# Two attention units scored singly instead of as a pair, and one value tile issued ahead of the mask build

## The chip, the cores and the metric

One core of one Trainium2 chip. Names in the profiles: PE is the matrix engine (PEld its weight loads), ACT the scalar engine, DVE the vector engine, POOL the general engine, which also issues most of the loads here; PSUM is the memory that PE writes to. The metric is the device time of one execution in microseconds (us), lower is better. The time of an execution is some 1.7 us longer than the profile's span.

## The reference, cut to what matters

```python
# q, k, v: (8 batches, 8 heads, 576 positions, 64), float32
scores = q @ k.T / 8
scores = where(abs(i - j) <= 32, scores, -1e9)      # sliding window
attn = softmax(scores) @ v
x = attn, heads side by side: (4608, 512)
h = x @ w_in                                        # w_in (512, 2048)
out = (h / (1 + exp(-1.702 * h))) @ w_out           # w_out (2048, 512)
```

## The kernel before

The 4608 rows are cut into 36 units of 128 rows, each of two blocks of 64 queries. A block needs 128 keys: the first block of a unit finds their values in the unit's own value tile (`ve`), the second in a shifted copy (`vo`) that takes 64 rows from each of two neighbouring tiles. From unit 10 on two units are scored together ("pair"), because their middle keys are shared. The order of instructions on each engine is the order of the program.

```python
def scores(self, u, ...):                 # single form; 32 products for 4 head pairs
    sc[u] = two PSUM banks (eo = even / odd heads), p[u] = [128, 2, 8, 64]
    ...
                        nc.tensor.matmul(sc[eo][lo:lo + 64, n, :], self.kT[r, hp, at:at + 64],
                                         self.qT[r, ..., q0:q0 + 16], ...)      # 64 x 64 x 64
    for eo in range(2):
        nc.scalar.activation(p[:, eo, cols], sc[eo][:, cols], AF.Exp, scale=self.scale)

def band(self, u, ...):                   # 2 mask products of 128 x 512, one for each eo
    ...

def scores_pair(self, a, kinds):          # 40 products, most of them 64 x 64 x 128
    sc = four PSUM banks (g = half of the head pairs, eo), each for BOTH units
    ...
    for (g, eo), src in sc.items():       # order (0,0) (0,1) (1,0) (1,1)
        nc.scalar.activation(p[:, eo, 2 * g:2 * g + 2], src, AF.Exp, scale=self.scale)

def band_pair(self, a):                   # 2 mask products of 128 x 1024: all heads of one eo, both units
    ...

def values_pair(self, us, kinds):         # 16 products for the first unit, then 16 for the second
    ...

def head(self):                           # the opening
    ... keys and queries of the first 512 rows are loaded
    for m in range(2):
        self.load_v(m)
    self.setup_mask()                     # POOL: one memset, four affine selects
    self.load_v(2, 0, 64)                 # the half tile
    for c in "kq":
        self.load_edge(c)
    self.load_w_in(0)
    self.load_v(2, 64); self.load_v(3); self.load_v(4, 0, 64)
    for c in range(1, 4):
        self.load_w_in(c)                 # second, third, fourth quarter of w_in
    ...
        self.layer1(0, 2)                 # needs the second quarter
        self.x_T(2, "t")
        self.layer1(0, 3)
        self.x_T(3, "o")
        self.layer1(0, 4)                 # the first step that needs the third quarter
        for d in range(4):
            self.layer1(1, d)             # need the first and second quarter

def window_4(self):
    ...
    run(l1)                               # last step of layer 1
    self.scores_pair(10, "aaaa")
    self.band_pair(10)                    # then window 5: layer 2 of unit 6, values_pair((10, 11)), scores_pair(12)
```

The softmax here doesn't subtract the row's maximum and nothing guards it: scores larger than these inputs give would overflow.

Of the kernel before, what the change touches and what calls it, by code (L numbers as in the profile page):

```python
# [23 lines left out]
RING = 1536  # L24
# [3 lines left out]
class _Kernel:  # L28
# [206 lines left out]
    def scores(self, u, hps=range(4), kinds="aa"):  # L235

        nc = self.nc
        if u not in self.p:
            self.sc[u] = [self.bank(kinds[eo], [128, 8, SQ], F32, f"sc{eo}") for eo in range(2)]
            self.p[u] = self.work.tile([128, 2, 8, SQ], BF16, name="p", tag="p", bufs=4)  # L240
        sc, p = self.sc[u], self.p[u]
        for hp in hps:
            for blk in range(2):
                n = 2 * hp + blk
                k0 = (128 * u + 64 * blk) % RING
                q0 = (128 * u + 64 * blk + 32) % RING // JT
                for half in range(2):
                    lo, at = 64 * half, k0 + 64 * (half ^ blk)
                    for eo in range(2):
                        r = slice(eo * 64, eo * 64 + 64)  # L250
                        nc.tensor.matmul(sc[eo][lo:lo + 64, n, :], self.kT[r, hp, at:at + 64],  # L251
                                         self.qT[r, JT * hp:JT * hp + JT, q0:q0 + 16],
                                         start=(hp in (0, hps[0]) and blk == 0), stop=(hp == hps[-1] and blk == 1))
        cols = slice(2 * hps[0], 2 * hps[-1] + 2)
        for eo in range(2):
            nc.scalar.activation(p[:, eo, cols], sc[eo][:, cols], AF.Exp, scale=self.scale)  # L256
# [76 lines left out]
    def values_pair(self, us, kinds):  # L333

        nc, D = self.nc, self.D
        acc = [self.bank(kind, [128, (7, 7, 2)[i], D + 1], F32, f"pv{i}") for i, kind in enumerate(kinds)]
        p = self.p.pop(us[0])
        for i, u in enumerate(us):
            for h in range(self.H):
                out, n = (acc[i], h) if h < 7 else (acc[2], i)  # L340
                for blk in range(2):
                    vt = (self.ve, self.vo)[blk][u % NV]
                    nc.tensor.matmul(out[blk * 64:blk * 64 + 64, n, :], p[:, h % 2, h // 2, 2 * i + blk, :],  # L343
                                     vt[:, h, :D + 1], start=(h in (0, 7)), stop=(h in (6, 7)))
            self.acc[u] = (acc[i], acc[2], i)

# [117 lines left out]
    def head(self):  # L464

        nc, dve, act = self.nc, self.nc.vector, self.nc.scalar
# [5 lines left out]
                self.load_heads(0, c, h)  # L472
        for m in range(2):
            self.load_v(m)
        self.setup_mask()
        self.load_v(2, 0, 64)
        for c in "kq":
            self.load_edge(c)
        self.load_w_in(0)
# [149 lines left out]
    def window_4(self):  # L629

        nc, dve, act = self.nc, self.nc.vector, self.nc.scalar
        l2 = [(lambda u=u, i=i: self.layer2(u, i, "oh"[u % 2], (dve, act)[u % 2])) for u in (4, 5) for i in range(4)]
        l1 = [(lambda d=d: self.layer1(3, d)) for d in range(8)]

        def run(lst, n=1):
            for _ in range(n):
                lst.pop(0)()

        self.scores(7)
        self.scores(8)  # L640
        self.scores(9, kinds="th")
        self.keys_X(13)
        self.keys_X(14)
        run(l2, 3)
        self.band(7)
        run(l2)
        self.band(8)
        self.values(7)
        self.norm(7)
        self.gelu_table()  # L650
        self.band(9)
        run(l2, 3)
        self.values(8)
        self.values(9)
        self.x_T(7, "t", act)
        self.norm(8)
        self.x_T(8)
        self.norm(9)
        self.x_T(9)
        self.loads(4)  # L660
        run(l2)
        run(l1, 2)
        for hp in range(4):
            self.pair_heads("q", 3, hp, dve)
        run(l1, 1)
        for hp in range(4):
            self.queries_T(3, hp, "t", act)
            run(l1)
        self.queries_wrap(3)
        self.feed(4)  # L670
        run(l1)
        self.scores_pair(10, "aaaa")
        self.band_pair(10)

    def window(self, w):

# [106 lines left out]
```

## Time and profile before

| Profile of the kernel before (span 306.2 us) | us |
|---|---|
| half value tile landed | 15.21 |
| third quarter of w_in landed | 24.66 |
| PE starts the step that needs it | 24.90 |
| first score product of unit 10 | 80.67 |
| first score product of unit 12 | 86.25 |
| from there to the end | 219.95 |

Landings are from the trace's completion records: a transfer is landed when the last of its 16 transfer engines has reported. The other rows are starts of PE instructions. The table splits the run into an opening (to unit 10), the stretch that part 1 changes (unit 10 to unit 12: 5.58 us), and the rest.

### The profile page before, as it was taken

How to read it: one execution, taken by the hardware profiler on the slowest of the kernel's cores; microseconds unless marked ns; L12 is line 12 of the kernel's file. 1: busy time of each engine (PE TensorE's matmuls, PEld its weight loads, DVE VectorE, ACT ScalarE, POOL GpSimd, SP SyncE). 2: the span in 40 equal slices, each digit the busy share in tenths (PEclk: the TensorE clock that was granted, in tenths of full speed). 3: DMA queues.
4: the chain of work that ended last, by engine and by line, in shares of the span. 5: the costliest groups of instructions: out<-in, count | busy, mean ns of one | idle time of the engine just before them, and what ended most of it. 6: DMA issues, size and time to landing. Idle time of an engine off the chain costs nothing.

```text
span 306.2 us, 8062 instructions
## 1 busy us (share of the span) xinstructions
PE 295.0 (96%) x3405; PEld 204.7 (67%) x3405; DVE 132.2 (43%) x389; ACT 181.3 (59%) x310; POOL 128.5 (42%) x186
## 2 busy tenths in 40 slices
PE   8689999999999999999999999999999999999992
PEld 5469765867657676767676767676767676766852
DVE  3763178766280627072707270717070708140011
ACT  3585554795857575757575757575756567414410
POOL 8873454796325282627252625252331301130120
PEclk9979999999999999999999999999999999999997
DMA  7999999999999999999999999999999525151112
GB/s 133 162 193 205 197 186 178 174 166 154 161 167 142 106 117 146 139 141 126 153 163 126 121 147 181 108 119 154 130 66 89 57 48 72 34 65 41 37 31 72
DMA packets 130324, 38.33 MB, mean 125 GB/s; under 512 B 111280, under 2 KB 128048, under 8 KB 130288
## 3 DMA queue, kind: packets, MB, share of 16 engines
q0 software_dynamic: 90032, 27.46, 95.5%
q1 hardware_dynamic: 40112, 10.30, 36.9%
q8 instruction: 26, 0.43, 0.6%
q14 instruction: 10, 0.08, 0.1%
q10 hardware_dynamic: 144, 0.07, 0.1%
HBM read 36.96 MB, written 9.44 MB: 152 GB/s over the span
## 4 chain that ended last, share of the span: by engine, by line
PE 90%; ACT 2%; POOL 2%; DMA 2%; DVE 1%; issue 0%; POOLq 0%; ACTq 0%
PE h_ps L395 40%; PE o_ps L419 39%; PE pv L343 3%; PE sc L285 2%; DMA ve<-in_v_dram 2%; PE tp L170 1%; PE o_ps L444 1%; PE pv L329 1%; PE sc L251 1%; PE tp L380 1%; ACT g L389 1%; POOL ve L142 1%; POOL ks L136 1%; ACT pp L289 1%; POOL qs L136 0%; POOL mask L97 0%
## 5 line engine op out<-in xcount | busy, mean ns | idle before, releaser
L395 PE MATMUL h_ps<-xT,w_in_sb 128*128 128x256 bf16 (+1 forms) x1168 | 130.6, 271 | 0.0
L419 PE MATMUL o_ps<-w_out_sb,g 128*128 128x512 bf16 x560 | 127.8, 379 | 0.0
L395 PEld LDWEIGHTS <-w_in_sb 128*128 128x128 bf16 x1168 | 112.3, 98 | 16.2 <-DVE xT L108 0.3
L389 ACT ACTIVATE g<-h_ps 128x512 bf16<-128x512 f32 x142 | 84.7, 597 | 60.8 <-PE h_ps L395 60.7
L431 POOL DMA_DIRECT2D out_dram<-o_sb x70 | 44.1, 634 | 148.1 <-DVE rec L353 73.7
L419 PEld LDWEIGHTS <-g 128*128 128x128 bf16 x560 | 53.0, 98 | 57.8
L108 DVE COPY o_sb<-o_ps 128x512 f32<-128x512 f32 x34 | 23.4, 690 | 126.1 <-PE o_ps L419 126.1
L289 ACT ACTIVATE pp<-sc 128x512 bf16<-128x512 f32 x48 | 24.8, 602 | 25.3 <-PE sc L285 25.3
L142 POOL DMA_DIRECT2D ve<-in_v_dram x41 | 35.5, 869 | 9.1 <-DMA w_out_sb<-in_moe_w_out_dram 3.6
L149 POOL DMA_DIRECT2D kn<-in_k_dram x27 | 23.4, 872 | 2.8 <-DMA w_out_sb<-in_moe_w_out_dram 1.5
L108 DVE COPY vo<-ve 64x528 bf16<-64x528 bf16 x69 | 22.0, 319 | 2.2 <-DMA ve<-in_v_dram 0.3
L354 DVE TENSOR_TENSOR x<-pv,rec 128x448 bf16<-128x448 f32 (+1 forms) x52 | 22.1, 425 | 1.9
L452 ACT ACT_TABLE_LOAD x13 | 16.7, 1283 | 0.2
L108 ACT COPY qT<-tp 128x512 bf16<-128x512 bf16 (+1 forms) x16 | 9.1, 569 | 9.2 <-PE tp L170 6.3
L455 ACT ACT_TABLE_LOAD x11 | 14.1, 1283 | 0.2
L136 POOL DMA_DIRECT2D qs<-in_q_dram x17 | 12.2, 727 | 4.5 <-DMA w_out_sb<-in_moe_w_out_dram 1.6
L256 ACT ACTIVATE p<-sc 128x512 bf16<-128x512 f32 (+1 forms) x24 | 10.8, 530 | 2.7 <-PE sc L251 2.7
L343 PEld LDWEIGHTS <-pp 128*64 128x64 bf16 x416 | 7.8, 110 | 6.2 <-issue 5.1
L108 DVE COPY kT<-tp 128x512 bf16<-128x512 bf16 (+1 forms) x13 | 8.5, 659 | 6.0 <-PE tp L170 4.4
L108 DVE COPY qc<-qs 128x512 bf16<-128x512 bf16 x32 | 9.2, 331 | 2.0 <-DMA qs<-in_q_dram 2.0
L306 DVE TENSOR_TENSOR pp<-pp,mask 128x1024 bf16<-128x1024 bf16 x14 | 9.0, 684 | 2.3 <-ACT pp L289 2.3
L343 PE MATMUL pv<-ve,pp 128*64 128x65 bf16 x208 | 9.3, 196 | 0.5 <-DVE pp L306 0.4
(74 smaller groups left out, 180.3 us busy)
## 6 DMA issues: line engine op xcount, KB each, us to landing
out_dram<-o_sb POOLq DMA_DIRECT2D x70, 128.0 KB, 5.8
ve<-in_v_dram POOLq DMA_DIRECT2D x31, 128.0 KB, 8.0
kn<-in_k_dram POOLq DMA_DIRECT2D x21, 128.0 KB, 8.1
w_in_sb<-in_moe_w_in_dram POOLq DMA_DIRECT2D x4, 512.0 KB, 9.0
w_out_sb<-in_moe_w_out_dram POOLq DMA_DIRECT2D x4, 512.0 KB, 13.2
qs<-in_q_dram POOLq DMA_DIRECT2D x2, 448.0 KB, 14.7
qs<-in_q_dram POOLq DMA_DIRECT2D x3, 256.0 KB, 7.7
qs<-in_q_dram POOLq DMA_DIRECT2D x2, 384.0 KB, 11.7
```

Source lines behind the costliest of these rows:

```text
L108: (eng.copy if eng is self.nc.scalar else eng.tensor_copy)(out, in_)
L136: self.nc.gpsimd.dma_start(self.stage[key][off // JT:(off + m) // JT, lo:hi, :], src[b, lo:hi, s:s + m, :].rearrange("h (p j) d -> p h (j ...
L142: self.nc.gpsimd.dma_start(self.ve[m % NV][at:at + n, :, :self.D], self.v[b, :, s:s + n, :].rearrange("h s d -> s h d"))
L149: self.nc.gpsimd.dma_start(kn[off:off + n], self.k[b, :, s:s + n, :].rearrange("h s d -> s h d"))
L289: nc.scalar.activation(p[:, eo, 2 * g:2 * g + 2], src, AF.Exp, scale=self.scale)
L343: nc.tensor.matmul(out[blk * 64:blk * 64 + 64, n, :], p[:, h % 2, h // 2, 2 * i + blk, :], vt[:, h, :D + 1], start=(h in (0, 7)), stop=(h ...
L354: nc.vector.tensor_mul(x[:, hs, :], src[:, :, :D], rec[:, hs, :].to_broadcast([128, hs.stop - hs.start, D]))
L389: self.nc.scalar.activation(self.g[t][:, 2 * d:2 * d + 2, :], hps, AF.Gelu_apprx_sigmoid)
L395: self.nc.tensor.matmul(hps[:, i, cols], self.w_in_sb[:, kr, ff * 128:(ff + 1) * 128], self.xT[t][:, kr, cols], start=(first and i == 0 an ...
L419: nc.tensor.matmul(o_ps, self.g[t][:, ff, s * 128:(s + 1) * 128], self.w_out_sb[:, ff, :], start=(ff == 0), stop=(ff == self.NFF - 1))
L431: self.nc.gpsimd.dma_start(self.out[row + 64 * blk:row + 64 * blk + 64, :].rearrange("(s j) f -> j s f", j=JT), o_sb[64 * blk:64 * blk + 64])
L452: self.nc.scalar.activation(self.spark, self.spark, AF.Gelu_apprx_sigmoid)
```

## The change

Part 1: units 10 and 11 use the single form (needs a wrap of the key ring, and `values_pair` takes two softmax tiles). The intent is that unit 10 can be masked before unit 11 is through the exponentials. Part 2: the half value tile is issued ahead of the mask build, so that it lands earlier.

```diff
-                    lo, at = 64 * half, k0 + 64 * (half ^ blk)
+                    lo, at = 64 * half, (k0 + 64 * (half ^ blk)) % RING
... values_pair:
+        pair = us[1] not in self.p
         p = self.p.pop(us[0])
         for i, u in enumerate(us):
+            if i and not pair:
+                p = self.p.pop(u)
...
-                    nc.tensor.matmul(out[...], p[:, h % 2, h // 2, 2 * i + blk, :],
+                    pq = p[:, h % 2, h // 2, 2 * i + blk, :] if pair else p[:, h % 2, h // 2 * 2 + blk, :]
+                    nc.tensor.matmul(out[...], pq,
... head:
+        self.load_v(2, 0, 64)
         self.setup_mask()
-        self.load_v(2, 0, 64)
... window_4:
-        self.scores_pair(10, "aaaa")
-        self.band_pair(10)
+        for u in (10, 11):
+            self.scores(u)
+            self.band(u)
```

More of the change, by code (lines that the diff above doesn't have):

```diff
@@ L342, in values_pair @@
                     vt = (self.ve, self.vo)[blk][u % NV]
-                    nc.tensor.matmul(out[blk * 64:blk * 64 + 64, n, :], p[:, h % 2, h // 2, 2 * i + blk, :],
+                    pq = p[:, h % 2, h // 2, 2 * i + blk, :] if pair else p[:, h % 2, h // 2 * 2 + blk, :]
+                    nc.tensor.matmul(out[blk * 64:blk * 64 + 64, n, :], pq,
                                      vt[:, h, :D + 1], start=(h in (0, 7)), stop=(h in (6, 7)))
```

## The prediction

> **What bounds the kernel now.** I read the page first, then the chain that ended last in order of time, then the timeline of the two places that the change touches. The page, parts 1, 2 and 4:
>
> ```profile
> PE 295.0 (96%) x3405; PEld 204.7 (67%) x3405; DVE 132.2 (43%) x389; ACT 181.3 (59%) x310; POOL 128.5 (42%) x186
> ...
> PE   8689999999999999999999999999999999999992
> ...
> PE 90%; ACT 2%; POOL 2%; DMA 2%; DVE 1%; issue 0%; POOLq 0%; ACTq 0%
> ```
>
> PE is on the chain for 90% of the span. In the 40 slices (7.66 us each) it is below 9 only in the first three. So a change can shorten the run only where PE still stands idle. Busy time on the other engines is free.
>
> From about 90 us there is nothing to win: the stretch 90.10 to 105.33 (one window of two units) shows PE busy for all of its 15.23 us.
>
> ```profile
> 90.10:105.33 15.23, 15.23 (x170) 10.44 (x169) 5.86 (x16) 9.81 (x17) 6.13 (x8) 1.00 1.45 126
> ```
>
> The columns are length, then busy us (and instructions) of PE, PEld, DVE, ACT and POOL. The PE clock of 1.00 says it is not throttled. Because PE is dense from here to the end, whatever is saved before 90 us arrives whole at the end.
>
> The chain just before shows the place where units 10 and 11 are scored (columns: start us, us, what):
>
> ```profile
> 80.78 0.60 ACT g L389
> ...
> 81.39 1.28 ACT L289
> ...
> 82.69 1.58 ACT pp L289 x3
> ...
> 84.30 1.30 DVE pp L306 x2
> ...
> 85.64 0.67 PE pv L343 x30
> 86.31 0.60 PE sc L285 x30
> 86.91 3.56 PE o_ps L419 x16
> ```
>
> Here the chain leaves PE: last gelu, table load, exponentials, mask products, and only then PE's value products. Meanwhile PE runs the 16 layer-2 products of unit 6. The last of them starts at 84.52, and at 216 ns apart PE is free at 84.73. The timeline shows it waiting for the mask products:
>
> ```profile
> 84.30 1.29 DVE L306 TENSOR_TENSOR pp<-pp,mask 128x1024 bf16<-128x1024 bf16 x2 [2.33 <-ACT pp L289]
> 85.04 0.11 PEld L343 LDWEIGHTS <-pp 128*64 128x64 bf16 x2 [0.64 <-DVE pp L306]
> ...
> 85.64 0.56 PEld L343 LDWEIGHTS <-pp 128*64 128x64 bf16 x30 [0.49 <-DVE pp L306]
> ```
>
> Two products start at 85.04 (head 0, after the first mask product), the other 30 at 85.64 (after the second). So about 0.9 us of PE time is lost, from 84.73 to 85.64.
>
> The opening has the other wait. The timeline, with the idle time before each row and its releaser in brackets:
>
> ```profile
> 4.68 1.77 POOL L142 DMA_DIRECT2D ve<-in_v_dram  x2
> ...
> 6.85 1.55 POOL L97 TENSOR_SCALAR_AFFINE_SELECT mask<-mask 64x128 bf16<-64x128 bf16 x4
> ...
> 8.36 0.70 POOL L142 DMA_DIRECT2D ve<-in_v_dram  x1
> ...
> 15.29 0.63 ACT L108 COPY vo<-ve 64x528 bf16<-64x528 bf16 x1 [0.89 <-DMA ve<-in_v_dram]
> ```
>
> The chain has a link "DMA ve<-in_v_dram" from 8.36 to 15.21, with the mask build on POOL ahead of it. This is what the second part of the change aims at.
>
> **What the Trainium skill says.** (1) "DMA: Bandwidth & Descriptors", section "Two DMAs through the same engine are not ordered": within one queue of one DMA engine descriptors start in order. The trace agrees: the tiles land in the order of issue, value tile 0 at 12.07, tile 1 at 13.12, the half of tile 2 at 15.21, the two edge loads at 15.42 and 15.62. (2) "TensorEngine Tiling (Array Packing)", "Key Properties": different tiles of the array work in parallel. That matters because "TensorE: Matmul & The Clock Gate", "Back-to-back issue gap", gives a floor of about 25 ns for small products, which would make 24 extra products cost 0.6 us. The trace overrules it: units 4 and 5 were scored singly, 64 products in 0.67 us, 10.5 ns each. (3) "Runtime: NRT & Kernel Launch", "Instruction fetch mechanics": instructions come in 16 KiB blocks by DMA. The trace has such packets, 16384 bytes each; the first starts at 12.86 and takes 1.22 us on one DMA engine.
>
> **Part 1, single scoring of units 10 and 11.** PE: the pair form has 40 score products, from 80.67 to 81.27, 0.60 us. The single form has 2 x 32 = 64, of half the width at most; measured for 64, 0.67 us. That is +0.07 us on PE, and layer 2 of unit 6 then leaves PE free at 84.80 instead of 84.73.
>
> ACT: four exponentials of 128x512 and one table load either way, so the ends stay at 83.29, 83.77, 84.26 and 84.75 (starts 82.69 to 84.14). The start is set by the gelu of 80.78 plus the 1.28 us load, not by the score products, which are over by 81.4. What changes is which tile each one holds. In the pair form each mask product covers both units for one half of the heads and needs exponentials 1 and 3, or 2 and 4; the first can start only at 84.30. In the single form exponentials 1 and 2 are unit 10, 3 and 4 unit 11.
>
> DVE: two products of 128x1024 (688 ns mean) become four of 128x512, 424 ns in this kernel's single units. That is 1.70 against 1.38 us busy, but each starts some 0.03 us after its own exponential and fits its 0.48 us pace: ends 83.74, 84.22, 84.71, 85.20. DVE was idle for 2.33 us before, so nothing is pushed.
>
> PE: unit 10 is masked at 84.22 and starts its 16 value products when PE is free, 84.80 (their PSUM bank was read by an exponential ending 84.75 at the latest). At 0.62/32 = 19 ns each they end at 85.11. Unit 11, head 0 follows; head 1 needs the last mask product, 85.20 plus the 0.05 us that the trace shows from DVE to PE, 85.25. Fourteen more at 20 ns: next scores at 85.54. Before, they started at 86.25. **Gain 0.7 us**: 0.9 us of waiting falls to some 0.1, less 0.07 of extra products. The other effects (48 more PE instructions with the weight loads, a different softmax buffer) touch no wait: the build's order shows the same waits with the new names.
>
> **Part 2, the earlier load.** POOL issues the half tile at 6.45 instead of 8.36, and the mask build (1.93 us from 6.43) moves behind it, ending at about 9.1 instead of 8.40. All issues from the edge loads (9.04) on keep their times.
>
> The load gains nothing that I can see. The queue is backed up when it is issued: keys and queries land at 9.51 and 11.04, value tiles after them. The trace's completion records per DMA engine show the fastest engine finishing tile 1 at 10.79 and the half tile at 11.22. That is 0.43 us for its 32 pieces at 13 ns, no gap. The descriptors were already waiting in line, in the same place as they will be. The late landing is one engine of 16: fifteen were done by 13.61, the last at 15.21, held by the instruction fetch of 12.86. An earlier issue moves neither.
>
> The mask's delay costs nothing either. The first mask product on DVE moves from 8.80 to about 9.13 and the four end near 10.2; the key copy behind them slips from 10.01 by 0.2 us, ends near 11.5, and the next DVE work waits until 11.76 anyway. **Sum of part 2: 0.0 us.**
>
> Total: 307.19 - 0.7 = 306.5 us; I put it at 306.45, with a little credit for rival A.
>
> **Rivals.** A: the half tile does land early, near 13.6, because its last piece on the slow engine slips in before the fetch. Then ACT's copy starts at 14.41, right after the one before it, 0.88 us sooner, and so do unit 1's value products. For it: in the trace that engine seems to have had about one piece left. Against full effect: layer 1 then meets its weights. The second quarter lands at 22.15 (used at 22.69), the third at 24.66 (used at 24.90), so at most 0.25 us gets past. Time: 306.2.
>
> B: the mask becomes the wait in the opening, because POOL runs it slower beside other work. DVE has 0.3 us of slack before 11.76; beyond that each 0.1 us would cost up to 0.1. Time: 306.6 to 306.9.
>
> C: part 1 gives nothing: the 24 extra products cost 0.6 us as the 25 ns floor says, or unit 10's value bank waits for something later than 84.8. The 10.5 ns of units 4 and 5 speak against the first, the ACT times against the second. Time: about 307.1.
>
> D: the gain is lost later to a transfer that PE then waits for. In 90 to 300 us no PE wait for a DMA appears, and the next key and value tiles land at 82 to 85 us for use after 87. Unlikely; time 307.2.
>
> **Range and chances.** The executions of before spread from 307.16 to 307.72, and the opening hangs on one DMA engine against one instruction fetch, good for some 0.3 us either way. So 305.9 to 307.0. Two per cent would be 6 us, seven times all idle time that the change touches: within 2% is near certain.
>
> **What would show it.** Right: exponentials in unchanged places relative to the last gelu, mask products of about 424 ns one behind each, unit 10's value products directly behind layer 2 with no wait, a wait of about 0.1 us in unit 11, the score products of units 12 and 13 some 0.7 us sooner; in the opening the half tile issued near 6.4 but landing near 15.2. Wrong: landing near 13.6 with unit 1's products moved (A), DVE waiting past 11.76 (B), score products near 1.2 us (C), or new PE waits after 90 us (D).

## More of the kernel before

One more view of the kernel before, stretches of the opening (length; busy us and instructions of PE, PEld, DVE, ACT, POOL; clock of PE; DMA share; GB/s):

```profile
12.00:17.00 5.00, 2.96 (x104) 2.35 (x104) 3.68 (x14) 3.57 (x9) 3.72 (x6) 0.89 1.68 170
17.00:20.00 3.00, 3.00 (x62) 2.39 (x61) 1.50 (x6) 2.04 (x5) 2.91 (x8) 0.61 1.39 205
```

PE stood still for two of the five microseconds, and its clock fell to 0.61 after it.

## The result, and the profile after

The changed kernel took 306.27 us in the median (306.06 to 306.60, 4 runs), the kernel before 307.40 beside it (307.16 to 307.72, 4 runs); ratio 0.9964, interval 0.9946 to 0.9981. Ratios are the mean time of one kernel's fast runs over that of the other's of the same rounds, so not quite the ratio of the medians. Executions over 1.5% slower than the fastest of the same kernel are left out of the means. The changed kernel had 21 fast runs with mean 306.64 and median 306.39, against 307.41 and 307.18 for the 52 of before: 0.77 us less in the mean, with a standard error of some 0.18 (standard deviations 0.71 and 0.69).

| | before | changed | difference |
|---|---|---|---|
| half value tile landed | 15.21 | 12.79 | |
| third quarter of w_in landed | 24.66 | 23.59 | |
| first score product of unit 10 | 80.67 | 79.42 | -1.25 |
| unit 10 to unit 12 | 5.58 | 4.94 | -0.64 |
| unit 12 to the end | 219.95 | 220.00 | +0.05 |
| span | 306.2 | 304.4 | -1.8 |

The two profiles differ by more than the two kernels do, and two thirds of it lies in the opening, where I had expected nothing. Part 1 first. The chain of the changed kernel around unit 10 (start us, us, what; line numbers are 4 higher than before in this part of the program):

```profile
79.50 0.67 PE sc L251 x64
80.16 0.16 issue
80.32 3.40 PE o_ps L423 x15
83.72 0.71 PE pv L347 x32
84.43 0.60 PE sc L285 x30
```

ACT and DVE have left the chain: layer 2 (`o_ps`) is followed by the value products (`pv`) and these by the next score products (`sc`). (The 0.16 of "issue" is a missing record: 15 of the 16 layer-2 products are in the trace.) The timeline shows the exponentials, the mask products and the weight loads of the value products (start us, busy us, engine, line, operation, output<-inputs, shapes, count, and in brackets the idle time before and what ended it):

```profile
81.44 2.06 ACT L256 ACTIVATE p<-sc 128x512 bf16<-128x512 f32 x4
82.07 1.89 DVE L265 TENSOR_TENSOR p<-p,mask 128x512 bf16<-128x512 bf16 x4 [0.99 <-ACT p L256]
83.65 0.67 PEld L347 LDWEIGHTS <-p 128*64 128x64 bf16 x32 [0.42 <-DVE p L265]
```

All 32 weight loads of the value products are one group now, where before there were 2, then a wait, then 30. The idle time that the page puts down to DVE there is mostly not a wait: from the start of the last 512-wide layer-2 product to the first value product it is 309 ns, and it is 309 or 310 ns in all 16 other places of the trace where layer 2 is followed by value products, before and after. Where layer 2 is followed by layer 1, which uses the array in the same form, it is 215 or 216 ns (16 places in each of the two traces). In the kernel before it was 524 ns here, and 0.6 us more followed between the second and the third product. Inside the changed stretch one gap of 0.08 us is left: the first product of unit 11 starts at 84.02, just after the end of the last mask product at 83.96.

After that PE is dense, as before (two records of PE are missing in this stretch):

```profile
88.30:103.53 15.23, 15.12 (x168) 10.43 (x169) 5.86 (x16) 9.81 (x17) 6.13 (x8) 1.00 1.92 151
```

Now the opening. The half tile is the third of one group of issues, and ACT's two copies follow each other without the wait of before:

```profile
4.63 2.50 POOL L142 DMA_DIRECT2D ve<-in_v_dram  x3
...
7.52 1.56 POOL L97 TENSOR_SCALAR_AFFINE_SELECT mask<-mask 64x128 bf16<-64x128 bf16 x4
...
13.35 1.28 ACT L108 COPY vo<-ve 64x528 bf16<-64x528 bf16 x2
...
23.63 0.44 PEld L399 LDWEIGHTS <-w_in_sb 128*128 128x128 bf16 x5 [0.27 <-DMA w_in_sb<-in_moe_w_in_dram]
```

The last line is the one that matters: PE waits for the third quarter of w_in (landed 23.59) and starts at 23.63. So the time at which the opening ends is set by a weight load, not by the half tile. But in this profile transfers that were issued long before the moved one were ahead too: the second part of the keys landed at 8.47 instead of 9.51. The change cannot have done that, which made me suspect the scatter rather than the change.

### The profile page after: what moved, and what is told of

It reads as the page before. It is cut to its first block, busy times and chain, and to the rows that moved or that the text cites. A ratio compares the mean times of both kernels' runs of the same rounds, so it can differ in the third digit from the quotient of the medians.

```text
span 304.4 us, 8079 instructions
## 1 busy us (share of the span) xinstructions
PE 291.9 (96%) x3395; PEld 203.8 (67%) x3429; DVE 132.5 (44%) x391; ACT 181.2 (60%) x310; POOL 128.6 (42%) x186
## 4 chain that ended last, share of the span: by engine, by line
PE 89%; POOL 4%; DMA 3%; issue 1%; ACT 1%; DVE 0%; POOLq 0%
PE h_ps L399 40%; PE o_ps L423 40%; DMA w_in_sb<-in_moe_w_in_dram 3%; PE pv L347 3%; PE sc L285 2%; POOL ve L142 2%; PE tp L170 1%; PE o_ps L448 1%; PE sc L251 1%; PE pv L329 1%; POOL ks L136 1%; POOL qs L136 0%; POOL w_in_sb L112 0%; POOL mask L97 0%; POOL edge L221 0%
## 5 line engine op out<-in xcount | busy, mean ns | idle before, releaser
L423 PE MATMUL o_ps<-w_out_sb,g 128*128 128x512 bf16 x526 | 125.3, 379 | 1.8 <-issue 0.2
L289 ACT ACTIVATE pp<-sc 128x512 bf16<-128x512 f32 x44 | 22.7, 602 | 24.7 <-PE sc L285 24.7
L256 ACT ACTIVATE p<-sc 128x512 bf16<-128x512 f32 (+1 forms) x28 | 12.8, 541 | 2.7 <-PE sc L251 2.7
L265 DVE TENSOR_TENSOR p<-p,mask 128x512 bf16<-128x512 bf16 (+1 forms) x28 | 9.8, 381 | 4.7 <-ACT p L256 2.3
L347 PEld LDWEIGHTS <-pp 128*64 128x64 bf16 x384 | 7.1, 110 | 5.1 <-issue 5.1
L465 PE MATMUL junk<-idle 128*128 128x256 bf16 x41 | 7.9, 333 | 1.5 <-DVE ve L88 1.1
## 6 DMA issues: line engine op xcount, KB each, us to landing
qs<-in_q_dram POOLq DMA_DIRECT2D x2, 384.0 KB, 10.5
```

Of the source, the lines that this page charges most:

```text
L347: nc.tensor.matmul(out[blk * 64:blk * 64 + 64, n, :], pq, vt[:, h, :D + 1], start=(h in (0, 7)), stop=(h in (6, 7)))
L423: nc.tensor.matmul(o_ps, self.g[t][:, ff, s * 128:(s + 1) * 128], self.w_out_sb[:, ff, :], start=(ff == 0), stop=(ff == self.NFF - 1))
```

## The experiments

**Theory 1 (as predicted):** part 1 is worth a fixed 0.6 to 0.7 us, part 2 nothing; the opening scatters, whatever the order of the two. **Rival (order of issue):** the earlier issue of the half tile is worth about 0.5 us. **Theory W**: the opening ends when the third quarter of w_in lands.

**One part at a time, and both kernels again.** Each of the two edits is the diff above with the other part left out; the other two are the kernels themselves.

```diff
 e1_single_only: part 1 alone                    e2_load_only: part 2 alone
         self.setup_mask()                       +        self.load_v(2, 0, 64)
         self.load_v(2, 0, 64)                            self.setup_mask()
-        self.scores_pair(10, "aaaa")            -        self.load_v(2, 0, 64)
+        for u in (10, 11): ...                           self.scores_pair(10, "aaaa")
```

> Part 1 alone (units 10 and 11 scored singly, the half value tile still loaded behind the mask build). As predicted: 0.7 us under the kernel before, ratio 0.9977, with the first score product of unit 12 about 4.9 us after the first of unit 10 (before: 5.58 us). If the single scoring were the whole gain: ratio 0.9964, and the kernel with part 2 alone at 1.000. If the opening were the whole gain: ratio 1.000.

> Part 2 alone (half value tile loaded ahead of the mask build, pair scoring kept). My prediction (the load waits in line anyway, its issue time does not count): ratio 1.000, the half tile lands at a time that scatters as in the kernel before. Rival (the order of issue decides): ratio about 0.9985, that is 0.45 us, the half tile lands near 12.8 us and unit 10 is scored near 79.4 us instead of 80.7.

> The kernel before, unchanged, for a second profile and for the scatter. Ratio 1.000 within 0.001. If the opening of the two profiles differs by luck (one transfer engine held by an instruction fetch), this profile can show the half tile landing anywhere from 12.8 to 15.2 us and unit 10 scored from 79.4 to 80.7; if the order of issue decides, it lands near 15.2 and unit 10 is scored near 80.7 again.

> The changed kernel, unchanged, for a second profile and as the yardstick of this call. Ratio 0.9964, equal to the sum of the two parts alone. By luck: the half tile can land as late as 15.2 us here; by order of issue: near 12.8 us again.

| | time, median (range) | ratio, interval | half tile landed | third quarter landed | unit 10 scored | unit 10 to 12 |
|---|---|---|---|---|---|---|
| part 1 alone | 307.22 (306.27 to 308.02) | 1.0005, 0.9986 to 1.0023 | 14.14 | 23.72 | 79.55 | 4.93 |
| part 2 alone (5 fast runs; a slow one, 312.91, left out; the profile is the slow one's) | 307.43 (307.16 to 309.35) | 1.0022, 1.0000 to 1.0043 | 13.28 | 23.89 | 79.72 | 5.58 |
| before again | 308.10 (306.80 to 310.09) | 1.0021, 1.0001 to 1.0040 | 13.81 | 25.68 | 82.86 | 5.57 |
| changed again | 306.53 (306.24 to 306.90) | 0.9983, 0.9971 to 0.9995 | 13.02 | 24.30 | 80.13 | 4.94 |

The stretch from unit 10 to unit 12 follows part 1 and nothing else, to 0.01 us. The opening follows neither part: with the load in its old place unit 10 was scored at 79.55 in one profile and at 82.86 in another, 3.3 us apart. The kernel before, compared with itself, came out at 1.0021 with an interval that leaves out 1.000: the intervals of five rounds may understate the scatter here, and no single ratio decides about half a microsecond. The times were misses for part 1 alone (no gain) and for the changed kernel (0.9983, expected 0.9964).

In four of these six profiles (both kernels' first ones counted) one number stands out: unit 10 was scored 55.83 us after the third quarter landed. That is theory W. The exceptions are the first profile of before (56.01: there PE itself was late, 0.24 us after the landing) and its second one (57.18). In that one PE waited for the second quarter, and its clock fell (PE timeline, and stretches as above):

```profile
23.21 1.79 PE L395 MATMUL h_ps<-xT,w_in_sb 128*128 128x256 bf16 x8 [1.35 <-DMA w_in_sb<-in_moe_w_in_dram]
```

```profile
22.00:24.00 2.00, 0.79 (x5) 0.59 (x6) 1.48 (x6) 0.00 (x0) 0.55 (x1) 0.84 1.24 206
24.00:26.00 2.00, 2.00 (x13) 1.56 (x12) 0.42 (x1) 0.60 (x1) 0.32 (x2) 0.50 1.24 206
```

Eight products took 1.79 us here and 1.04 at full clock. So the late quarters cost their own delay here and then another 1.4 us. The trace's clock records have one stretch at half clock in this opening, 3.41 us long (from 23.35); in the first profile of before there is one of the same length from 15.94, after a wait of 1.51 us.

The profile of part 2 alone fell into a slow run (312.91). It shows rival D of the prediction: in window 6 PE waited for a key transpose by DMA, and the 16 layer-2 products after it took 6.21 us instead of 3.63, with the clock at 0.50 to 0.58.

```profile
103.58 0.91 PE L285 MATMUL sc<-qT,kT 64*64 64x64 bf16 x32 [2.31 <-DMA kT<-kn]
```

It appeared in one profile of fourteen, in a slow run, so nothing is concluded from it about the change; it says only that in one execution a transfer of a later window was not hidden.

**Does the half tile count, or the weights (second call)?** Three kernels ran with five rounds; the fourth, with the quarters swapped, ran once, for its profile (state unknown, as for every single run).

```diff
 e5_half_first                       e8_quarters_swapped
+        self.load_v(2, 0, 64)      -        for c in range(1, 4):
         for m in range(2):         +        for c in (1, 3, 2):
             self.load_v(m)                      self.load_w_in(c)
-        self.load_v(2, 0, 64)
         self.setup_mask()          e6: part 1 alone again; e7: the changed kernel again
```

> The changed kernel with the half value tile put at the head of the value loads, ahead of tiles 0 and 1. If the opening ends when the third quarter of the first weight matrix lands (theory W: in four of five good profiles the first score product of unit 10 came 55.83 us after that landing), the half tile's place is of no account: same mean as the two kernels beside it, ratio about 0.998. If the half tile's landing is what the opening hangs on, this one is surely early (near 11.3 us) and is at least as fast as the changed kernel: 0.9965 or less.

> Part 1 alone once more, for the scatter (first call: 306.27 to 308.02). Theory W and luck: mean within 0.3 us of the changed kernel of this call. Order of issue: again 0.6 to 0.8 us slower than it. In the profile the stretch from the first score product of unit 10 to that of unit 12 is 4.94 us in either case.

> The changed kernel a third time. Part 1 is worth a fixed 0.64 us (5.58 to 4.94 us in every profile so far), ratio 0.9979; what is beyond that is the opening. Order of issue: 0.9964 again, and its runs within 1 us of each other. Luck: anywhere from 0.996 to 1.000, mean near 0.998.

> The changed kernel with the third and fourth quarter of the first weight matrix loaded in the other order, so that the third lands some 3 us later (near 26.7 instead of 23.6 us). Theory W: the first score product of unit 10 comes 55.83 us after its landing, near 82.5 us instead of 79.4 to 80.1, and the time rises by about 3 us to some 309.3. If the opening hangs on the half value tile: no change, 306.3.

| | time, median (range) | ratio, interval | third quarter landed | unit 10 scored | difference |
|---|---|---|---|---|---|
| half tile first | 306.22 (306.09 to 306.94) | 0.9968, 0.9943 to 0.9993 | 23.71 | 79.54 | 55.83 |
| part 1 alone | 306.25 (306.02 to 308.13) | 0.9976, 0.9948 to 1.0004 | 23.65 | 79.48 | 55.83 |
| changed | 306.67 (306.01 to 308.14) | 0.9982, 0.9955 to 1.0009 | 23.68 | 79.51 | 55.83 |
| quarters swapped | 310.73 (1 run) | | 26.86 | 84.11 | 57.25 |

Part 1 alone, with the load in its old place, now ran like the changed kernel beside it (306.02 against 306.01 at best) and had the same opening (79.48 against 79.51). In the profile with the half tile first, it landed at 11.57, 1.3 us sooner than in the changed kernel beside it (12.86), and the opening was no sooner for it (79.54 against 79.51 beside it). Swapping the quarters settles theory W: the third quarter landed 3.2 us later and PE stood until then.

```profile
26.91 1.46 PE L399 MATMUL h_ps<-xT,w_in_sb 128*128 128x256 bf16 x6 [3.23 <-DMA w_in_sb<-in_moe_w_in_dram]
```

```profile
26.00:28.00 2.00, 1.09 (x6) 0.79 (x7) 0.00 (x0) 0.00 (x0) 0.69 (x1) 0.61 1.25 206
28.00:30.00 2.00, 2.00 (x12) 1.43 (x11) 0.00 (x0) 0.60 (x1) 0.87 (x1) 0.54 1.25 204
```

The delay was 1.4 us more than the expected sum, again with one stretch of 3.41 us at half clock after the wait (from 26.43).

**What part 1's gain is made of, and a version that needs the weights later.**

```diff
 e9_mask_swapped                     e10_third_later
         for u in (10, 11):                  self.layer1(0, 2)
             self.scores(u)                  self.x_T(2, "t")
-            self.band(u)           +        self.x_T(3, "o")
+        for u in (11, 10):                  self.layer1(0, 3)
+            self.band(u)           -        self.x_T(3, "o")
                                    -        self.layer1(0, 4)
 e11: the changed kernel again               for d in range(4):
                                                 self.layer1(1, d)
                                    +        self.layer1(0, 4)
```

> The changed kernel with the mask products of unit 11 put ahead of those of unit 10; the same instructions otherwise. If the gain of part 1 is that unit 10 is masked early and PE starts its value products then, it is lost and more: unit 10 is masked last, about 5.38 us after the first score product of unit 10, and the first score product of unit 12 follows at about 6.03 us after it (changed kernel 4.94, kernel before 5.58). If the gain came from the smaller score or mask products as such: 4.94 us still.

> The changed kernel with the layer-1 step that first needs the third weight quarter moved behind four steps of the next pair, which need the first two quarters alone, and the two transposes put together. Theory W: unit 10 is no longer scored at landing + 55.83 us; in a good profile near 79.4 us as before, in a poor one (third quarter after 24 us) up to 1 us sooner than that sum. Time: at or below the changed kernel of this call, ratio 0.996 to 0.998, with fewer runs over 307. If the third quarter's landing were not what the opening waits for: the same mean and the same scatter as the changed kernel.

> The changed kernel, as the yardstick of this call: mean 306.6 as over its 15 runs so far, ratio near 0.998; 4.94 us from the first score product of unit 10 to that of unit 12; unit 10 scored 55.83 us after the landing of the third weight quarter if that lands before about 24.4 us.

With the masks swapped (one run, 306.93 us, state unknown; read by its stretch, not by its time) the stretch from unit 10 to unit 12 was 5.86 us (79.43 to 85.29): longer than in the kernel before, with the same instructions as the changed kernel. The mask products start late, and PE waits for them:

```profile
83.06 1.59 DVE L265 TENSOR_TENSOR p<-p,mask 128x512 bf16<-128x512 bf16 x4 [2.36 <-ACT p L256]
84.38 0.14 PEld L347 LDWEIGHTS <-p 128*64 128x64 bf16 x2 [1.14 <-ACT p L256]
84.69 0.56 PEld L347 LDWEIGHTS <-p 128*64 128x64 bf16 x30 [0.18 <-DVE p L265]
```

So the gain needs the order: unit 10 through the mask while unit 11 is still in the exponentials. (I expected 6.03; four mask products with nothing between them took 1.59 us, 0.40 each, less than the 0.42 I had used.)

The version that needs the third quarter later took 306.14 us (305.69 to 306.99), ratio 0.9964, interval 0.9939 to 0.9990; the changed kernel beside it 306.32 (306.09 to 308.92), ratio 0.9983, interval 0.9949 to 1.0018. In its profile the wait for the third quarter is gone:

```profile
21.04 1.05 PE L399 MATMUL h_ps<-xT,w_in_sb 128*128 128x256 bf16 x8 [0.42 <-DMA w_in_sb<-in_moe_w_in_dram]
...
22.53 4.64 PE L399 MATMUL h_ps<-xT,w_in_sb 128*128 128x256 bf16 x41
```

Unit 10 was scored at 79.17, 55.67 us after the third quarter's landing (23.50), so 0.16 us sooner than by the sum; the second quarter (landed 20.99) is what PE waits for now. It had the fastest single runs. Its mean, 306.26 over 6 runs, against 306.64 over 21 of the changed kernel, with standard errors of 0.24 and 0.15, does not prove it faster.

**The half tile last.**

```diff
-        self.load_v(2, 0, 64)
         self.setup_mask()
         for c in "kq":
             self.load_edge(c)
+        self.load_v(2, 0, 64)
```

> The changed kernel with the half value tile issued last: behind the mask build and behind the two edge loads, near 10.4 us instead of 6.4. If only the place in line counts and the opening ends with the third weight quarter (theory W), the half tile lands with the edge loads, near 14 us, ACT's copy of it (free from about 14.1) hardly waits, unit 10 is scored at landing of the third quarter + 55.83 us, and the mean stays at 306.5 to 306.9, ratio near 0.998. If an early issue of the half tile is worth something by itself, this one must be worse than part 1 alone (mean 306.92 over 12 runs): above 307.2, ratio 1.000 or more.

It took 306.56 us (306.39 to 307.18), ratio 0.9977, interval 0.9964 to 0.9991; mean 306.64 over 5 runs, exactly the changed kernel's mean over its 21. In its profile the half tile landed at 14.42 (issued at 9.70), ACT's copy waited until 14.49, and still unit 10 was scored 55.84 us after the third quarter (24.80 to 80.64). An issue 3 us later than in the changed kernel costs nothing that shows. PE waited once for 1.19 us in this opening (from 21.16), with no half clock after it: here the late quarter cost its own delay alone.

All fast runs of the kernels that differ only in part 1 and in the place of the half tile say together how much is left for part 2. I take the 0.64 us of part 1 off the runs that still score in pairs. Then 69 runs with the half tile behind the mask build have a mean of 306.79 and 32 with it ahead 306.66: 0.13 us apart, with a standard error of 0.15. The rival's 0.5 us falls. In ten profiles unit 10 was scored 55.83 or 55.84 us after the third quarter landed; the four others are the two of before, the swapped quarters, and the version made not to wait for it.

## Why the prediction was right or wrong

The time (306.27 against 306.45) and the verdict were right, and part 1's mechanism with them. That the time came within 0.2 us is partly luck (last point). Its steps:

- **PE is the bound and dense from 90 us on, so a gain before it arrives whole.** Right: 219.95 and 220.00 us from unit 12 to the end. The slow run of part 2 alone is the exception to keep in mind. One reading was wrong: PE is below 9 in the last slice as well (2), after its last product at 300.5 us, where the change touches nothing.
- **Part 1: four exponentials in unchanged places, mask products of 0.42 us each behind its own, 0.07 us more for 64 products.** Right: 1.91 us from the start of the last gelu to the first exponential in both profiles, mask products of 425 ns, 0.67 us for the 64 score products (so rival C is out), and the swapped masks show that the gain needs the order of the mask products. A detail was off: unit 11 waited before its head 0, not before head 1.
- **"PE free at 84.80", and from it a gain of 0.7 us.** A term too small: I let PE go on 216 ns after the start of the last layer-2 product. It is 309 ns to the first value product, wherever PE does not wait for a mask. "TensorEngine Tiling (Array Packing)", section "Key Properties", says that a change of tiling mode drains the engine; I had read that section for the parallel tiles only. The trace agrees: 309 ns against the 215 or 216 to a product of the same form. The missing 0.09 us falls on the changed kernel alone, because in the kernel before the wait for the mask covered it. 0.71 less 0.09 is near the 0.64 measured.
- **Part 2: "Sum of part 2: 0.0 us".** Right as far as the times tell: half tile first, in its new place, in its old place and last gave means of 306.34 (6 runs), 306.64 (21), 306.92 (12) and 306.64 (5). The first three rise with the time of issue, but the latest issue breaks the row; and in the one call with the first three side by side the old place (306.63) beat the new one (306.82), with half tile first at 306.34. The mask build was no wait either (rival B): in the first profile of the changed kernel the first mask product on DVE started at 9.12, with 9.13 forecast.
- **"An earlier issue moves neither" (neither the place in line nor the late landing).** Not borne out as a statement on the landing. In eight profiles with the load ahead of the mask and in line behind tiles 0 and 1, it landed at 12.50 to 13.28; in four with the load behind the mask at 13.05 to 15.21. It seems to land earlier, and I cannot say why. It does not matter for the end, because PE waits for weights later on: what I had as the limit of rival A ("layer 1 then meets its weights") is the rule and not the exception. By the prediction's own list, the sign of rival A did appear in the recorded profile: the half tile landed at 12.79, and unit 1's products waiting for it started at 14.69 instead of 15.97. But with the load in its old place they started at 14.97 and 14.77 (part 1 alone, two profiles), so it was not the mark of the change.
- **The landing at 15.21 as a property of the kernel.** Wrong: it was one execution. I explained it by an instruction fetch that coincided with the late engine; fetches of the same size stand in all profiles between 10.97 and 12.86, mostly without such an effect. The cause was argued, not shown. The 0.3 us allowed for the opening was too little: over two profiles of the unchanged kernel unit 10 was scored at 80.67 and 82.86.
- **The 1.1 us of the comparison** are 0.64 of part 1 and some 0.5 of opening: the changed kernel's four runs there have a mean of 306.30, 0.34 below its mean over 21 runs, while the four of before are at their usual mean (307.42). That half is luck: the forecast gave it 0.05 us at most, and part 1's 0.7 us alone, taken from the 307.40 beside it and not from the earlier 307.19, would have given 306.7.

What stays open: why in some executions one of the 16 transfer engines falls 1 to 2 us behind (in the second profile of before it completed the first quarter of w_in at 18.57 when the other 15 were done by 16.64), and whether the earlier half tile makes poor openings rarer. The quarter of w_in that stands third in line landed after 24.4 us in three of the five profiles with the half tile behind the mask build (24.66, 25.68, 24.80) and in none of the nine with it ahead (23.50 to 24.30), too few to decide. Part 1 alone and the changed kernel differ by 0.28 us in the mean with a standard error of 0.28, which neither shows nor excludes it.

## What to carry to other kernels

When a wait is a chain of exponentials and mask products for two units, group the work so that the first unit is through the whole chain while the second is still in its first stage; more and smaller instructions on PE and DVE cost less than the wait if those engines have room (here 0.07 us of PE and 0.3 of DVE, against 0.9 us of waiting). Before crediting an opening to a moved load, take a second profile of the unchanged kernel: find the landing that PE waits for last, and check whether the start of the dense part keeps a fixed distance from it over several profiles. Price a wait on PE together with its clock: in two openings waits of 1.35 and 3.23 us were followed by 3.41 us at half clock, which added 1.4 us each time; a wait of 1.19 us in another was not.

## What the Trainium skill lacked or had wrong

- "TensorE: Matmul & The Clock Gate", "Back-to-back issue gap": the floor of about 25 ns that its table gives for small products can't be used for products that go to different 64 x 64 tiles of the array: 64 of them took 0.67 us, 10.5 ns each. The page's own part on packing (section "Measured speedup vs the span model") has about 4 ns from tile to tile, and in the trace four products follow each other by 3 or 4 ns, the next four some 20 ns later; the table does not point to it.
- "TensorEngine Tiling (Array Packing)", "Key Properties": the drain at a change of mode has no figure there. Here 309 ns lie between the start of the last 512-wide product and the first value product on half the columns, against 216 ns from one 512-wide product to the next: 93 ns.
- "Runtime: NRT & Kernel Launch", "Instruction fetch mechanics": the 16 KiB blocks agree (16384-byte packets); the page treats the fetch as mostly hidden and does not say how long a block takes: 0.89 to 1.42 us in the first 45 us of these profiles. Whether this delays the data behind it is not settled here.
- No page read gives a figure for how far apart the 16 engines of one transfer finish: for the half tile 1.9 us from the first to the last in the first profile of the changed kernel and 4.0 in that of before, for the first quarter of w_in 3.1 us in the second profile of before.
